# Loads of w_in in written order, |w| of the later weights on VectorE, and g2's tap and edges on GpSimd, in a three-layer float32 kernel

## The chip, the cores and the metric

The kernel runs on one core of a Trainium2 chip. The metric is device time in microseconds (us) for one execution. PE is TensorE, DVE is VectorE, ACT is ScalarE, POOL is GpSimd and SP is SyncE, whose queue issues nearly all transfers.

## The reference

Three layers follow each other, for 4 batches of 576 positions and 512 channels (8 heads of 64):

```python
# layer 1: attention, causal, window 128, with a linear bias per head
scores = scale * q @ k.T
scores = where((rel >= 0) & (rel < 128), scores + bias, -1e9)
attn = exp(scores - max); attn = attn / (attn.sum(-1) + 1e-9)
x = attn @ v                                    # heads side by side: 576 x 512
# layer 2: gated MLP with a spatial gate
h = gelu(x @ w_in)                              # 512 x 1024
u, v = h[..., :512], h[..., 512:]
v_n = (v - mean) / sqrt(var + 1e-6) * g_ln
v_s = w_sg @ v_n + b_sg                         # over the positions
x = x + (u * v_s) @ w_out
# layer 3: gated linear unit with a convolution over 3 positions
h = relu(x @ w_in2)                             # 512 x 1024
conv = conv_w[0] * h[s-1] + conv_w[1] * h[s] + conv_w[2] * h[s+1]
out = (h * sigmoid(conv)) @ w_out2              # 1024 x 512
```

The weights come in 64-bit floats; all else is float32.

## The kernel before

**Precision.** Each float32 operand of layers 2 and 3 is held as a high and a low part in a shorter float format, and a product is made of three matmuls (high by high, low by high, high by low). The names carry it: `xh`/`xl`, `gh`/`gl`, `vn`, `x2g` (high and low of the input of layer 3), `gr` (the 64 positions left over of `gg`, called the edge).

**Weights.** `narrowed` (L244 to L262) takes a piece of a 64-bit weight by DMA (L249), makes |w| from its high words (on ACT at L255 or on DVE at L257, by booked load), clamps it (L259) and puts sign and bits together in three more DVE operations (L260 to L262). The high part is then written on POOL (L181), the low part is a subtraction, mostly on POOL (L187). `w_in` comes in 8 pieces of 512 columns: `i1.k` are the halves that V uses, `i0.k` those that U uses. `w_out` has 8 pieces (`o`), `w_in2` and `w_out2` 32 pieces of 256 columns (`a`), which are written to DRAM (L308) and read back (L595) as the tiles `w2` and `wout2` when layer 3 needs them; in the trace tiles of `w_in2` read as `w`.

**Layer 1.** Heads go in pairs, four pairs a batch. L loads k and q (L321), M loads V (L325), C makes the scores on PE (`sc`, 20 matmuls a pair), DVE adds the bias and takes the maximum (L360), E takes exponentials on ACT (`t`), N norms, T transposes, A multiplies by V, X splits the result.

**Layer 2.** V.j makes `psv` and v (gelu on ACT, norm on DVE and POOL), U makes `psu` and u, G multiplies by `w_sg` (`pss`), W by `w_out` (`pso`) and writes the result x to DRAM (L549).

**Layer 3.** It reads x back (`x2s`, L607) and splits it into `x2g`. D (function `g2`) makes one block of 128 of the 1024 columns of h: 24 matmuls into `psg` (`psg2` in the program), relu into `hb`, the middle tap of the convolution (`scaled`, L198), two more taps on DVE (L645, L646), sigmoid on ACT, `gg` on DVE, its split into `gh` and `gl`, and the split of the edge into `gr0` and `gr1`. F (`g3`) multiplies by `w_out2`. There are 8 D units in each of 4 batches; three D units of batch 0 are run ahead, inside layer 2.

**Order.** Steps are written out by a list (`_steps`): batch 0's attention stands alone at the start; that of batch b+1 is woven into layer 2 of batch b. A list scheduler then moves instructions on each engine, except those that `tc.keep_in_program_order` holds. Which engine takes a flexible operation is chosen among those that the table `ON` allows, by booked loads. The stages of 64-bit pieces of `w_in` (tag `vn`) have 5 buffers, those of the smaller pieces 2, and each DMA waits for its buffer in SP's one queue.

The first steps as they are written:

```python
s = ["k0", "L0.0", "k2", "k1", "M0.0"] + scores(0) + loads(1) + ["i1.0"] + weigh(0) + scores(1) + loads(2) + ["i1.1"] + weigh(1)
...
s += back(2) + halves(2) + back(3) + halves(3) + ["k3"] + [f"i0.{k}" for k in range(4)]
```

Of the kernel before, what the change touches and what calls it, by code (L numbers as in the profile page):

```python
# [31 lines left out]
NA = 6  # L32
SLACK = 6000.0
# [6 lines left out]
    "tap": "act dve pool", "glu": "dve", "a hi": "act", "a lo": "pool",  # L40
    "edge hi": "act dve pool", "edge lo": "dve",
# [6 lines left out]
def _steps():  # L48
# [26 lines left out]
    s += back(2) + halves(2) + back(3) + halves(3) + ["k3"] + [f"i0.{k}" for k in range(4)]  # L75
    for b in range(B - 1):
# [5 lines left out]
        uv = V[:2] + loads(p) + scores(p) + V[2:] + loads(p + 1) + scores(p + 1) + U[0] + loads(p + 2) + U[1][:1] + scores(p + 2) + U[1][1:]  # L82
# [29 lines left out]
def attention_gmlp_glu_kernel(  # L112
# [185 lines left out]
    def w2_piece(i, c):  # L298
# [458 lines left out]
```

## Time and profile before

| | |
|---|---|
| median of 3 runs | 615.66 us (614.83 to 617.19) |
| profiled execution, its own time | 614.43 us |
| its span, first to last instruction | 612.4 us |
| mean granted clock of PE | 0.975 |
| PE busy | 562.5 us (92%) |
| DVE busy | 399.1 us (65%) |
| ACT busy | 244.7 us (40%) |
| POOL busy | 256.2 us (42%) |

The profile is of one execution. A busy time sums the instructions of an engine; what a wait costs is read from the stretch in which it stands. The times of the views below count from the start of the span.

### The profile page before, as it was taken

The page shows a single profiled execution, that of the slowest core. Times are in us where ns is not written, and L with a number is a line of the kernel's source. Part 1 is how long each engine was busy: PE and PEld are TensorE (multiplying, and loading weights), DVE is VectorE, ACT ScalarE, POOL GpSimd, SP SyncE. Part 2 cuts the span into 40 slices and gives each one's busy share as a digit, 9 for nine tenths or more (in the row PEclk, how much of TensorE's full clock was granted, in tenths as well). Part 3 has the DMA queues.
Part 4 walks back from the last instruction along what each step waited for, and adds up shares of the span by engine and source line. Part 5 has one row for each costly group of instructions (what it writes and reads, how often), then busy time and mean ns, then how long its engine had stood idle before and what let it go on. Part 6 is the DMA issues. An engine that isn't in the chain of part 4 may idle for free.

```text
span 612.4 us, 10380 instructions
## 1 busy us (share of the span) xinstructions
PE 562.5 (92%) x3704; PEld 480.4 (78%) x3704; DVE 399.1 (65%) x981; ACT 244.7 (40%) x626; POOL 256.2 (42%) x403
## 2 busy tenths in 40 slices
PE   6499959799998999999999997996899999999998
PEld 3366649588778888779798897886789898998887
DVE  3877957454585885586875855759996666556600
ACT  4764107863026744127733211115445333334311
POOL 0763655962142741245542634425664223322310
PEclk9799969899999899999999999997999999999999
DMA  8733402141324144424235847662200100000011
GB/s 303 278 119 102 144 2 89 40 137 33 105 100 129 45 156 128 134 58 125 66 110 152 313 136 227 206 222 78 78 17 35 55 17 18 36 18 17 18 51 52
DMA packets 44851, 63.55 MB, mean 104 GB/s; under 512 B 4352, under 2 KB 27392, under 8 KB 44800
## 3 DMA queue, kind: packets, MB, share of 16 engines
q1 hardware_dynamic: 44656, 62.60, 31.5%
q8 instruction: 29, 0.48, 0.3%
q10 hardware_dynamic: 144, 0.29, 0.1%
q14 instruction: 22, 0.18, 0.1%
HBM read 45.05 MB, written 17.83 MB: 103 GB/s over the span
## 4 chain that ended last, share of the span: by engine, by line
PE 56%; DVE 17%; DMA 12%; POOL 5%; issue 4%; ACT 4%; SPq 0%; POOLq 0%; DVEq 0%; ACTq 0%
PE psg L168 26%; PE pso L168 6%; PE o L168 6%; PE sc L168 4%; PE psv L168 4%; PE pss L168 4%; DMA w<-in_w_in_dram 4%; PE pT L402 3%; DMA w<-in_w_out_dram 3%; DVE t L360 3%; DMA w2d<-w 3%; ACT t L142 2%; PE psu L168 2%; DVE wa L261 1%; DVE wa L259 1%
## 5 line engine op out<-in xcount | busy, mean ns | idle before, releaser
L168 PE MATMUL psg<-x2g,w 128*128 128x288 f32 x768 | 108.3, 297 | 0.1
L168 PEld LDWEIGHTS psg<-x2g,w 128*128 128x128 f32 x768 | 105.8, 190 | 2.1 <-ACT hb L641 0.3
L168 PE MATMUL psg<-wout,gh 128*128 128x512 f32 (+1 forms) x272 | 82.4, 387 | 8.0 <-ACT gh L177 8.0
L142 ACT ACTIVATE t<-t,mx 128x256 f32<-128x256 f32 (+1 forms) x144 | 67.2, 469 | 23.2 <-DVE mx L360 23.1
L168 PE MATMUL pss<-wsg,vn 128*128 128x256 f32 (+1 forms) x448 | 66.4, 304 | 7.0 <-DVE t L529 7.0
L168 PEld LDWEIGHTS pss<-wsg,vn 128*128 128x128 f32 x448 | 61.9, 194 | 8.7 <-DVE t L529 8.1
L168 PE MATMUL sc<-k,q 64*128 64x256 f32 (+2 forms) x320 | 53.7, 408 | 11.8 <-DMA q<-in_q_dram 6.3
L168 PEld LDWEIGHTS psg<-wout,gh 128*128 128x128 f32 x272 | 49.8, 190 | 18.8 <-ACT gh L177 8.9
L168 PE MATMUL psu<-xh,win 128*128 128x256 f32 (+1 forms) x256 | 54.9, 307 | 8.7 <-POOL win L181 5.9
L360 DVE CUSTOM_DVE_ANT_0 t<-sc,tab 128x256 f32<-128x256 f32 (+2 forms) x144 | 47.8, 379 | 17.3 <-PE sc L168 17.2
L168 PE MATMUL pso<-gh,wo 128*128 128x256 f32 (+1 forms) x256 | 55.0, 308 | 4.1 <-DVE t L529 1.6
L198 POOL TENSOR_SCALAR t<-t,r 128x256 f32<-128x256 f32 (+2 forms) x105 | 51.3, 506 | 14.0 <-DVE r L387 6.7
L181 POOL TENSOR_SCALAR gr<-gg 128x64 fp32r<-128x64 f32 x30 | 16.4, 547 | 94.8 <-DVE gg L187 94.8
L168 PEld LDWEIGHTS sc<-k,q 64*128 64x128 f32 (+1 forms) x320 | 30.2, 198 | 32.4 <-issue 13.5
L168 PE MATMUL psg<-wout,gl 128*128 128x512 f32 (+1 forms) x136 | 52.4, 385 | 1.3 <-POOL gl L187 1.3
L168 PEld LDWEIGHTS psu<-xh,win 128*128 128x128 f32 x256 | 42.7, 196 | 11.5 <-POOL win L181 6.4
L168 PE MATMUL psv<-win,xh 128*128 128x512 f32 (+1 forms) x160 | 49.9, 397 | 0.0
L168 PEld LDWEIGHTS pso<-gh,wo 128*128 128x128 f32 x256 | 40.6, 190 | 9.0 <-DVE x L187 2.1
L187 POOL TENSOR_TENSOR gl<-gg,gh 128x512 fp32r<-128x512 f32 x32 | 43.9, 1375 | 8.2 <-ACT gh L177 8.2
L168 PE MATMUL o<-ph,V 128*64 128x128 f32 (+2 forms) x448 | 41.3, 301 | 3.1 <-ACT ph L177 2.9
L198 DVE TENSOR_SCALAR cc<-hb,cw 128x576 f32<-128x576 f32 x30 | 20.3, 680 | 30.3 <-ACT hb L641 30.3
L181 POOL TENSOR_SCALAR w<-wa 128x256 fp32r<-128x256 f32 x32 | 13.7, 428 | 62.4 <-DVE wa L262 45.6
(78 smaller groups left out, 1053.6 us busy)
## 6 DMA issues: line engine op xcount, KB each, us to landing
w<-in_w_out_dram SPq DMA_DIRECT2D x24, 256.0 KB, 2.8
V<-in_v_dram SPq DMA_DIRECT2D x16, 320.0 KB, 3.5
k<-in_k_dram SPq DMA_DIRECT2D x16, 288.0 KB, 3.1
x2s<-x2d SPq DMA_DIRECT2D x16, 288.0 KB, 2.8
q<-in_q_dram SPq DMA_DIRECT2D x15, 288.0 KB, 3.5
w<-in_w_in_dram SPq DMA_DIRECT2D x8, 512.0 KB, 7.8
w<-in_w_in_dram SPq DMA_DIRECT2D x16, 256.0 KB, 2.9
w2d<-w SPq DMA_DIRECT2D x32, 128.0 KB, 2.0
```

The source lines that it names most:

```text
L142: ins = nc.scalar.activation(*args, **kw)
L168: nc.tensor.matmul(out, lhsT, rhs, start=start, stop=stop, **kw)
L181: nc.gpsimd.tensor_scalar(dst, src, 1.0, 1.0, op0=ALU.mult, op1=ALU.mult)
L187: (nc.vector if eng == "dve" else nc.gpsimd).tensor_tensor(dst, a, b, op=op)
L198: e.tensor_scalar(dst, src, col, 1.0, op0=ALU.mult, op1=ALU.mult)
L259: tc.keep_in_program_order(clamp.tensor_scalar(f(a), f(a), W_LOW, W_HIGH, op0=ALU.max, op1=ALU.min))
L261: nc.vector.scalar_tensor_tensor(a, high, 0xC0000000, a, op0=ALU.bitwise_and, op1=ALU.bitwise_or)
L360: nc.vector.tensor_tensor_reduce(e, banks[4 if i == 4 else (j, i // 2)][:, o : o + nk], tab[:, m, tc], scale=-SCALE, scalar=3e38, op0=ALU. ...
L402: nc.tensor.transpose(ps[:, n * P : (n + 1) * P], s["t"][:, c0 : c0 + P], ident)
```

## The change

The core of the diff:

```diff
-    "tap": "act dve pool", "glu": "dve", "a hi": "act", "a lo": "pool",
-    "edge hi": "act dve pool", "edge lo": "dve",
+    "tap": "act pool", "glu": "dve", "a hi": "act", "a lo": "pool",
+    "edge hi": "pool", "edge lo": "pool",
...
-    s += back(2) + halves(2) + back(3) + halves(3) + ["k3"] + [f"i0.{k}" for k in range(4)]
+    s += back(2) + halves(2) + back(3) + halves(3) + ["k3"]
...
+        if b == 0:
+            V = [x for k in range(4) for x in (f"i0.{k}", V[k])] + V[4:]
+            uv = V + loads(p) + U[0][:1] + scores(p) + U[0][1:] + loads(p + 1) + scores(p + 1) + loads(p + 2) + U[1][:2] + scores(p + 2) + U[1][2:]
...
+    idle = mpool.tile([P, 128], BF16, tag="v", name="idle", bufs=NV)
+    nc.vector.memset(idle, 0.0)
...
-        nc.sync.dma_start(st[:, : 2 * n], src)
+        dma = nc.sync.dma_start(st[:, : 2 * n], src)
+        if stag == "vn":
+            tc.keep_in_program_order(dma)
...
-        if pick(dict(act=52 + 0.85 * n, dve=67 + 0.52 * n)) == "act":
+        if stag == "vn" and pick(dict(act=52 + 0.85 * n, dve=67 + 0.52 * n)) == "act":
             tc.keep_in_program_order(nc.scalar.activation(f(a), f(high), AF.Abs))
         else:
-            nc.vector.tensor_scalar(a, high, 0x7FFFFFFF, None, op0=ALU.bitwise_and)
+            tc.keep_in_program_order(nc.vector.tensor_scalar(a, high, 0x7FFFFFFF, None, op0=ALU.bitwise_and))
...
-        a = narrowed(src, 256, pool, "wa", 2, pool, "w64", 2)
-        hi = staged[0][:, :256].bitcast(F32R)
+        a = narrowed(src, 256, *((mpool, "v", NV) if p2pool else (pool, "wa", 2)), pool, "w64", 2)
+        hi = pool.tile([P, 256], F32R, tag="wh", name="wh", bufs=1 if p2pool else 2)
...
+            if b and (j, i) == (0, 4):
+                tc.keep_in_program_order(ins)
...
+            if b and (j, i) == (1, 0):
+                tc.keep_in_program_order(ins)
...
+    ps = gps.tile([P, 512], F32, tag="g", name="idle")
+    for _ in range(NIDLE):
+        tc.keep_in_program_order(nc.tensor.matmul(ps[:, :128], idle, idle, start=True, stop=True))
```

`NIDLE` is 40. As built, ACT carries 9 of the |w| operations instead of 36 and DVE 27 more; all 32 middle taps are on POOL (L198 becomes L203, L181 and L187 become L186 and L192), as are all edges. The high part of a `w_in2` or `w_out2` piece goes to a tile of its own (`wh`) instead of its stage.

**SP's queue at the start.** Before, the rows from the first load of `w_in` (`w64` from `in_w_in`) to the q of the third pair of heads:

```order
L249 DMA w64_140<-in_w_in_dram 128x1024
L249 DMA w64_201<-in_w_in_dram 128x1024
L249 DMA w64_262<-in_w_in_dram 128x1024
L249 DMA w64_372<-in_w_in_dram 128x1024
L560 DMA gln_80<-in_g_ln_dram 128x4
L561 DMA bsg_81<-in_b_sg_dram 128x576
L249 DMA w64_570<-in_w_in_dram 128x1024
L249 DMA w64_1796<-in_w_in2_dram 128x512
L249 DMA w64_1890<-in_w_in2_dram 128x512
L321 DMA k_195<-in_k_dram 128x576
L321 DMA q_197<-in_q_dram 128x576
```

The same place after the change:

```order
L257 DMA w64_183<-in_w_in_dram 128x1024
L577 DMA gln_80<-in_g_ln_dram 128x4
L578 DMA bsg_81<-in_b_sg_dram 128x576
L257 DMA w64_1839<-in_w_in2_dram 128x512
L257 DMA w64_1934<-in_w_in2_dram 128x512
L330 DMA k_238<-in_k_dram 128x576
L330 DMA q_240<-in_q_dram 128x576
L330 DMA k_299<-in_k_dram 128x576
L330 DMA q_301<-in_q_dram 128x576
L330 DMA k_783<-in_k_dram 128x576
L330 DMA q_785<-in_q_dram 128x576
```

Four loads of `w_in` beyond the first stood ahead of the third pair's k and q (`k_195` and `q_197`, now `k_238` and `q_240`); now the next load of `w_in` comes behind these rows and one load of V.

**ACT around the first V steps.** Before, |w| of the four `i0` pieces and the gelus of V (`v` from `psv`):

```order
L255 ACTIVATE wa_572<-w64_570 128x512
L255 ACTIVATE wa_582<-w64_580 128x512
L255 ACTIVATE wa_592<-w64_590 128x512
L255 ACTIVATE wa_602<-w64_600 128x512
L142 ACT_TABLE_LOAD
L142 ACTIVATE v_624<-psv_610 128x512
L142 ACTIVATE v_650<-psv_636 128x512
L177 CAST wsg0_666<-wst_790 128x576
L177 CAST wsg0_666<-wst_848 128x576
L142 ACTIVATE v_716<-psv_702 128x512
L142 ACTIVATE v_742<-psv_728 128x512
```

After the change, from the first gelu to the first u:

```order
L147 ACTIVATE v_637<-psv_623 128x512
L147 ACTIVATE v_673<-psv_659 128x512
L147 ACTIVATE v_709<-psv_695 128x512
L147 ACTIVATE v_745<-psv_731 128x512
L264 ACTIVATE wa_651<-w64_649 128x512
L264 ACTIVATE wa_687<-w64_685 128x512
L147 ACTIVATE v_771<-psv_757 64x512
L264 ACTIVATE wa_723<-w64_721 128x512
L147 ACTIVATE u_808<-psu_795 128x256
```

Before, all four |w| stood ahead of the first gelu; now one of them (`wa_615`) does, and the other three stand behind the fourth gelu, the last of them behind the fifth.

**DVE and POOL at the first D units that follow layer 2.** Before, DVE's rows from the third `gg` on (`cc` is the convolution's sum, `gr1` the low part of the edge):

```order
L187 TENSOR_TENSOR gg_4759<-cc_4754,hb2_4641 128x576
L187 TENSOR_TENSOR gr1_4686<-gg_4679,gr0_4685 128x64
L187 TENSOR_TENSOR gr1_4686<-gg_4720,gr0_4685 128x64
L198 TENSOR_SCALAR cc_4793<-hb0_4639,cw_82 128x576
L198 TENSOR_SCALAR cc_4832<-hb1_4640,cw_82 128x576
L187 TENSOR_TENSOR gr1_4686<-gg_4759,gr0_4685 128x64
L645 SCALAR_TENSOR_TENSOR cc_4793<-hb0_4639,cw_82,cc_4793 128x576
L645 SCALAR_TENSOR_TENSOR cc_4832<-hb1_4640,cw_82,cc_4832 128x576
```

After the change, POOL's rows at that place:

```order
L203 TENSOR_SCALAR cc_4829<-hb2_4716,cw_82 128x576
L186 TENSOR_SCALAR x2g_5049<-x2s_5051 128x576
L186 TENSOR_SCALAR gr0_4760<-gg_4754 128x64
L192 TENSOR_TENSOR gr1_4761<-gg_4754,gr0_4760 128x64
L192 TENSOR_TENSOR gl_4757<-gg_4754,gh_4756 128x512
L203 TENSOR_SCALAR cc_4868<-hb0_4714,cw_82 128x576
L186 TENSOR_SCALAR gr0_4760<-gg_4795 128x64
L192 TENSOR_TENSOR gl_4798<-gg_4795,gh_4797 128x512
L186 TENSOR_SCALAR gr0_4760<-gg_4834 128x64
L203 TENSOR_SCALAR cc_4907<-hb1_4715,cw_82 128x576
```

The taps (`cc` from `hb`) and the low edges (`gr1`) left DVE and stand on POOL between the high edges (`gr0`) and `gl`.

On PE the three D units that are run ahead move forward in V of batch 3: before, 6 of their 72 matmuls stood ahead of the fifth `psv` group and the rest among U and G; now 54 of them stand ahead of the third `psv` group, and the other 18 between the fourth and the fifth.

## Rows read from the trace of the kernel before

**Rows 1.** Windows: length, busy us of each engine, granted clock, DMA share, GB/s.

```profile
0.00:20.00 20.00, 10.08 (x40) 5.55 (x40) 9.48 (x44) 9.69 (x33) 4.12 (x13) 0.97 0.92 324
...
60.00:80.00 20.00, 16.01 (x92) 10.97 (x90) 20.00 (x70) 3.04 (x5) 13.63 (x16) 1.00 0.35 113
...
80.00:95.00 15.00, 10.06 (x57) 9.17 (x57) 7.00 (x14) 2.63 (x7) 5.62 (x10) 0.66 0.00 0
...
120.00:340.00 220.00, 214.98 (x1562) 180.80 (x1559) 149.83 (x468) 96.84 (x284) 92.85 (x169) 0.99 0.34 107
...
400.00:420.00 20.00, 14.29 (x97) 13.67 (x95) 14.35 (x23) 9.00 (x15) 5.79 (x13) 0.86 0.61 201
...
420.00:450.00 30.00, 26.34 (x166) 23.86 (x165) 29.30 (x37) 12.40 (x22) 20.54 (x19) 0.98 0.17 48
```

**Rows 2.** Timeline, PE and ACT at the start: start, duration, operation, [idle before].

```profile
5.28 5.01 PE L168 MATMUL sc<-k,q 64*64 64x192 f32 x20 [5.28 <-DMA k<-in_k_dram]
...
10.50 5.07 PE L168 MATMUL sc<-k,q 64*64 64x192 f32 x20 [0.21 <-DMA q<-in_q_dram]
...
12.76 0.66 ACT L255 ACTIVATE wa<-w 128x512 f32<-128x512 f32 x1 [2.20 <-DMA w<-in_w_in_dram]
...
71.11 2.69 PE L168 MATMUL sc<-k,q 64*64 64x192 f32 x20 [0.19 <-DVE mx L360]
```

**Rows 3.** Chain of waits, first 125 us: start, duration, what.

```profile
6.63 8.68 DMA w<-in_w_in_dram
...
15.33 6.23 DMA q<-in_q_dram
...
87.62 11.36 PE psu L168 x72
```

**Rows 4.** Timeline, PE at the first U steps.

```profile
77.47 0.50 PE L168 MATMUL psu<-xh,win 128*128 128x256 f32 x2 [2.05 <-POOL win L181]
...
84.55 0.80 PE L168 MATMUL psu<-xh,win 128*128 128x256 f32 x2 [3.88 <-POOL win L181]
```

**Rows 5.** Timeline, SP, DVE, ACT and PE from 334 to 380 us.

```profile
335.98 3.21 SPq L595 DMA_DIRECT2D w<-w2d  x6
...
364.88 0.29 DVE L257 TENSOR_SCALAR wa<-w 128x256 uint32<-128x256 uint32 x1 [2.21 <-DMA w<-in_w_out_dram]
...
376.05 0.43 ACT L255 ACTIVATE wa<-w 128x256 f32<-128x256 f32 x1 [3.60 <-DMA w<-in_w_out_dram]
...
378.38 2.32 PE L168 MATMUL pss<-wsg,vn 128*128 128x320 f32 x14 [3.09 <-DVE t L529]
```

**Rows 6.** Timeline, POOL and PE at the change to layer 3.

```profile
412.03 0.67 POOL L181 TENSOR_SCALAR x2g<-x2s 128x576 fp32r<-128x576 f32 x1 [7.87 <-DMA x2s<-x2d]
...
418.13 2.07 PE L168 MATMUL psg<-wout,gh 128*128 128x512 f32 x4 [5.71 <-ACT gh L177]
```

**Rows 7.** Lines by form, 405 to 450 us: busy, mean ns, idle before.

```profile
L187 POOL TENSOR_TENSOR gl<-gg,gh 128x512 fp32r<-128x512 f32 x9 | 14.2, 1592 | 0.0
...
L645 DVE SCALAR_TENSOR_TENSOR cc<-hb,cw,cc 128x576 f32<-128x576 f32 x10 | 9.3, 950 | 0.6 <-POOL cc L198 0.6
...
L187 DVE TENSOR_TENSOR gr<-gg,gr 128x64 fp32r<-128x64 f32 x9 | 7.3, 827 | 0.1
...
L187 DVE TENSOR_TENSOR gg<-cc,hb 128x576 f32<-128x576 f32 x9 | 6.7, 753 | 0.0
...
L198 DVE TENSOR_SCALAR cc<-hb,cw 128x576 f32<-128x576 f32 x6 | 6.1, 1029 | 0.0
...
L198 POOL TENSOR_SCALAR cc<-hb,cw 128x576 f32<-128x576 f32 x2 | 2.6, 1309 | 0.0
```

**Rows 8.** One tile's view, gr on DVE: nanoseconds minimum, median, maximum.

```profile
L187 DVE TENSOR_TENSOR gr<-gg,gr x32: 211/1284/1322, 419.4 to 582.6; 128x64 fp32r<-128x64 f32 x32
```

**Rows 9.** Timeline, POOL and DVE at 445 us.

```profile
445.07 1.28 POOL L187 TENSOR_TENSOR gl<-gg,gh 128x512 fp32r<-128x512 f32 x1
...
445.14 1.29 DVE L187 TENSOR_TENSOR gr<-gg,gr 128x64 fp32r<-128x64 f32 x1
```

More of the change, by code (lines that the diff above doesn't have):

```diff
@@ L32 @@
 NA = 6
+NIDLE = 40
 SLACK = 6000.0
@@ L81, in _steps @@
         W = [[f"W{b}.{half}.{m}" for m in range(4)] for half in range(2)]
-        uv = V[:2] + loads(p) + scores(p) + V[2:] + loads(p + 1) + scores(p + 1) + U[0] + loads(p + 2) + U[1][:1] + scores(p + 2) + U[1][1:]
+        if b == 0:
+            V = [x for k in range(4) for x in (f"i0.{k}", V[k])] + V[4:]
+            uv = V + loads(p) + U[0][:1] + scores(p) + U[0][1:] + loads(p + 1) + scores(p + 1) + loads(p + 2) + U[1][:2] + scores(p + 2) + U[1][2:]
+        else:
+            uv = V[:2] + loads(p) + scores(p) + V[2:] + loads(p + 1) + scores(p + 1) + U[0] + loads(p + 2) + U[1][:1] + scores(p + 2) + U[1][1:]
         T, A = ([f"{x}{of(p + i)}" for i in range(4)] for x in "TA")
@@ L87, in _steps @@
         if b == 0:
-            s += weave(uv, [f"g{c}" for c in range(5)] + [f"o{k}.0" for k in range(4)]) + ["o0.1"] + gw[:2] + ["o1.1"] + gw[2:4] + ["o2.1"] + gw[4:6] + ["o3.1"] + gw[6:]
+            s += uv[:9] + weave(uv[9:], [f"g{c}" for c in range(5)] + [f"o{k}.0" for k in range(4)]) + ["o0.1"] + gw[:2] + ["o1.1"] + gw[2:4] + ["o2.1"] + gw[4:6] + ["o3.1"] + gw[6:]
         else:
@@ L167, in mm @@
         load["pe"] += book_pe
-        nc.tensor.matmul(out, lhsT, rhs, start=start, stop=stop, **kw)
+        return nc.tensor.matmul(out, lhsT, rhs, start=start, stop=stop, **kw)
     def copy(dst, src, psum=False, engines="act dve pool"):
@@ L241, in attention_gmlp_glu_kernel @@
     kept = {}
-    staged = []
     STAGE = dict(st=S, vn=1024, w64=512)
@@ L248, in narrowed @@
         st = spool.tile([P, STAGE[stag]], U32, tag=stag, name="w64", bufs=sbufs)
-        nc.sync.dma_start(st[:, : 2 * n], src)
-        staged[:] = [st]
+        dma = nc.sync.dma_start(st[:, : 2 * n], src)
+        if stag == "vn":
+            tc.keep_in_program_order(dma)
         words = st[:, : 2 * n].rearrange("p (n w) -> p n w", w=2)
@@ L353, in block @@
             out = banks[of][d if i == 4 else slice(0, P), o : o + nk]
-            mm(out, s["q"][d, q0 : q0 + nq], s["k"][d, k0 : k0 + nk], start=True, stop=True)
+            ins = mm(out, s["q"][d, q0 : q0 + nq], s["k"][d, k0 : k0 + nk], start=True, stop=True)
+            if b and (j, i) == (0, 4):
+                tc.keep_in_program_order(ins)
         def masked(j, i):
             o, nk = BLK[i][6], BLK[i][3]
-            e, c, tc = weights(s, j, i)
+            e, c, part = weights(s, j, i)
             book("dve", 80 + nk)
-            nc.vector.tensor_tensor_reduce(
-                e, banks[4 if i == 4 else (j, i // 2)][:, o : o + nk], tab[:, m, tc],
+            ins = nc.vector.tensor_tensor_reduce(
+                e, banks[4 if i == 4 else (j, i // 2)][:, o : o + nk], tab[:, m, part],
                 scale=-SCALE, scalar=3e38, op0=ALU.add, op1=ALU.min, accum_out=s["mx"][:, c : c + 1],
             )
+            if b and (j, i) == (1, 0):
+                tc.keep_in_program_order(ins)
         for j, i in ((0, 4), (1, 0), (0, 0), (1, 1), (0, 1)):
```

## The prediction

> **What bounds the kernel now.** I read the windows first. From 120 to 340 us PE is busy 214.98 of 220 us at a clock of 0.99, so there nothing but PE's own work could be saved beyond 5.0 us [rows 1]. The losses stand at two places. One is the first 95 us: PE idles 9.9 us of the first 20, 4.0 us from 60 to 80, and 4.9 us from 80 to 95, where the granted clock is 0.66, part of it at 1.2 GHz instead of 2.4. The other is the change to layer 3: 5.7 us idle from 400 to 420 and 3.7 us from 420 to 450 [rows 1]. In both, DVE is full beside an idle PE: 20.00 of 20 us from 60 to 80, 29.30 of 30 us from 420 to 450.
>
> Then the timeline of the start. The first 20 score matmuls take 5.01 us and the next 5.07 us; the same 20 take 2.69 us at 71 us [rows 2]. The ratio of 1.9 is near that of the two clock levels, though the window's clock column reads 0.97 there; I trust the durations. ACT's |w| of a `w_in` piece at 12.76 us stands among the exponentials and holds them for 2.20 us [rows 2]. The chain of waits then runs through a transfer of w_in from 6.63 us (8.68 us long) into the load of the third pair's q, which lands at 15.33 + 6.23 = 21.6 us. Its last step in this stretch is a run of 72 U matmuls from 87.62 to 98.98 us [rows 3].
>
> At 77.47 and 84.55 us U waits 2.05 and 3.88 us for `win`, the pieces i0 of w_in that POOL narrows late [rows 4]. Late in layer 2 a chain of the same kind shows once: |w| on ACT at 376.05 us, the load before it 3.60 us late, then PE at 378.38 us, idle 3.09 us [rows 5].
>
> At the change to layer 3 the first read of x lands at about 412 us, and PE resumes with `gh` at 418.13 us after 5.71 us of idleness [rows 6].
>
> **The change part by part.** The sum is made against the profiled execution's 614.43 us, which is 1.2 us under the median of 615.66 us.
>
> *Warm-up matmuls.* No row shows a 128-column matmul of this kind. The 72 U matmuls of 256 to 320 columns take 158 ns each, some cold [rows 3]; by columns that is 65 ns for 128, twice that cold, so 40 take 2.6 to 5.2 us. Begun at 1 us (a guess, no row shows it) they end between 3.6 and 6.2 us, and the first scores start at 5.28 us now, since they wait for k: nothing to 0.9 us lost. If the clock then stays up, the first scores save 5.01 - 2.69 = 2.3 us. The second 20 save as much, but behind them stands the third pair's q, so that is not added.
>
> The Trainium skill, page "TensorE: Matmul & The Clock Gate", Part 1 on the clock gate, gives 107 ns between cold matmuls of 128 columns; by it the estimate is 40 x 0.107 = 4.3 us and no delay.
>
> *Loads of w_in in written order.* Four pieces of 512 KB leave SP's queue ahead of the third pair's k and q. That is 2.1 MB; at the first window's 324 GB/s it is 6.5 us [rows 1], and the long load's own 8.68 us for what was queued with it is the upper bound [rows 3]. I take 5.5 us, as that window includes the 2 us before any load ran: q lands near 16 us instead of 21.6 us. Less if k and q then wait for their buffers, which the faster first scores free earlier. The exponentials of the pairs that follow start earlier by that, and the 2.20 us before 12.76 us fall away inside it.
>
> *i0 among the V steps.* Attention of batch 0 then ends earlier, and DVE, full from 60 to 80 us, has the same work: what starts 5.5 us earlier ends so. But three of the four |w| of i0 now stand on ACT behind the fourth gelu, where before all stood ahead of the first. What queues behind them is their clamp on DVE, the high part on POOL, and U on PE. If they come early enough, U's waits of 2.05 and 3.88 us go, and half of the 11.36 us run no longer runs cold (2 us more). If they come late, the lead is eaten. I take the lead of the load plus 1 us of U: **-6.5 us** (bounds: -14, all of the waits and the cold run gone; +2, three pieces of about 2 us each in series behind the last gelu, less the lead).
>
> *|w| of the later weights on DVE.* It is 27 more instructions of 0.29 us on DVE [rows 5], 7.8 us, hidden where DVE is idle (70 of 220 us from 120 to 340 [rows 1]). The exponentials lose the weights between them. From 120 to 340 PE can gain 5.0 us at most; I take **-1** (0 to -4). At 376 us the wait was for a load that stands behind larger loads of `wout`; with the high part in a tile of its own a stage comes free one POOL step earlier and the load is issued before them: **-2** (0 to -3.09).
>
> *D units run ahead.* 54 of their matmuls now follow two V groups of batch 3 instead of 6 following four. The loads of w2 are issued from 335.98 us [rows 5], behind the last part written to DRAM; two V groups are 24 matmuls of 512 columns, by the U run's 158 ns for some 290 columns [rows 3] about 7 us of PE. So that much of the cover that the loads had is gone: **+1** (0 to +7, if PE must wait for all but its first parts).
>
> *Tap and edges to POOL.* Now the DVE group from 405 to 450 us: nine units (the nine `gg`), with the low edge at 827 ns and six taps at 1029 ns; POOL's `gl` takes 1592 ns and its tap 1309 ns [rows 7]. DVE gives away about 0.83 + 0.69 = 1.5 us a unit. POOL, busy 20.54 of 30 us [rows 1], takes on at least 1.31 + 0.21 us a unit. Nine units in those 45 us are 5.0 us each; POOL's 20.54/30 of that, 3.4 us, plus 1.5 us is 4.9 us. One full engine is traded for another. Yet the low edge has two lengths, 211 ns at least and 1284 ns in the median [rows 8], and at 445.14 us it lasts just as long as the `gl` beside it [rows 9]: the two take turns, and on one engine that wait is gone. Bounds: -9.4 us if both waits of PE go (5.7 + 3.7), +5 if POOL's rows grow by a third of what it takes on. I take **-1.5**.
>
> Sum: -6.5 - 1 - 2 + 1 - 1.5 = -10, which is 604.4 us for the profiled execution and **605.5 us** on the median's scale.
>
> **The rivals.**
> *The lead is swallowed.* The three |w| behind the gelus set U's end, and the run of 72 still ends near 99 us. For it: DVE has no idle time from 60 to 80 us [rows 1]. Against: 5.5 us of DVE's work moves ahead. Without the 6.5 us: 612 us.
>
> *Everything comes.* U's waits go (2.05 + 3.88 us on top of the lead) and the first D units run at PE's pace (9.4 us instead of 1.5): 605.5 - 5.9 - 7.9 = 591.7 us. For it: DVE is full exactly where PE idles.
>
> *The w2 loads hold PE.* The full 7 us instead of 1: 611.5 us.
>
> *POOL and DVE exclude each other (slower).* The place is the D units from 402 us on. Rows 9 show one such turn. If it held for all of POOL's work and DVE's three operations over two tiles, a unit would take 1.31 + 0.21 + 0.24 + 1.28 on POOL plus two of 0.95 and 0.75 (and about as much for `x2g`) on DVE: 6.4 us, 0.24 being the high edge, taken a little over the low one's minimum. Nine take 57.6 us instead of 45: 605.5 + 1.5 + 12.6 = 619.6 us. It decides above 6.3 us a unit, where nine take 11.7 us more than now and use up the 8.5 us of the other terms and 3.1 us (0.5%) more. Against: `gg` with 753 ns in the mean can hardly hold turns of 1.28 us, and the low edge, which does, leaves DVE.
>
> The Trainium skill, page "SBUF — State Buffer", section "Who interferes with whom", states such a rule: a VectorE instruction with two inputs in SBUF and a GpSimd instruction that reads SBUF share a port pair, and the later one fully waits. Rows 9 agree with it; whether it holds so strictly for the long operations the rows leave open.
>
> **How the numbers follow.** About 0.5% is what a measurement of this kernel can tell from no change, so faster means under 612.6 us, slower over 618.7 us. Forecast 0.48 (its own range 598 to 611.5); lead swallowed 0.15; everything 0.17; w2 loads 0.09; exclusion 0.11. Faster: nearly all of the forecast, half of the swallowed, all of the next and two thirds of the w2 case: 0.46 + 0.08 + 0.17 + 0.06 = 0.77. Slower: 0.1, most of the exclusion. The rest, 0.13, is no change. The range reaches from everything (591) to the swallowed lead with a little exclusion (615).
>
> **What would show it.** First scores near 2.7 us and the third pair's q landing near 16 us show the start right. The U run ending at 92 to 93 us instead of 99 shows that the lead came through; waits of U on `win` behind ACT's |w| would show it swallowed. No idle PE at 376 us. In V of batch 3, PE waiting on transfers of w2 would be the w2 case. In the D units, POOL near 5 us a unit with PE idle 6 to 9 us from 400 to 450 is the forecast; more idle there is the exclusion, less is the gain. The prediction is wrong if the scores stay at 5 us (then it was not the clock), if the third pair's loads wait for buffers, or if a unit goes over 6.3 us.

## The result and the profile after

The changed kernel takes 620.96 us (median of 7 runs, 618.1 to 623.1) where the kernel before takes 615.87 us in the same series. The ratio is 1.007, with a 95% interval of 1.0045 to 1.0096: 0.7% slower (ratios, here and below, leave disturbed runs out, so they can differ a little from the quotient of two medians). The forecast was 605.5 us. The profiled execution took 618.1 us, its span is 616.3 us.

Where the time went is read by putting the same points of the program side by side: the start of the first instruction of each kind on PE, in the timelines of the two profiled executions.

| point of the program | before, us | after, us | after - before |
|---|---|---|---|
| last step of U done, first `pss` of batch 0 | 98.81 | 105.05 | +6.2 |
| first `pso` of batch 0 | 107.81 | 116.47 | +8.7 |
| first `psv` of batch 3 | 331.99 | 330.95 | -1.0 |
| first D unit behind layer 2 | 402.66 | 405.99 | +3.3 |
| first F matmul | 418.13 | 418.76 | +0.6 |
| end of the span | 612.4 | 616.3 | +3.9 |

So the lead of 6.5 us that was forecast for U's end is a loss of 6.2 us; the middle gives back nearly ten; and layer 3 with V of batch 3 ahead of it loses five again. The windows of the kernel after, with the columns of [rows 1]:

```profile
0.00:20.00 20.00, 14.01 (x98) 10.33 (x98) 10.79 (x52) 10.60 (x39) 5.83 (x16) 0.93 0.76 259
...
60.00:80.00 20.00, 13.43 (x53) 9.68 (x51) 15.55 (x29) 3.61 (x6) 11.33 (x19) 0.76 0.08 27
...
400.00:420.00 20.00, 16.55 (x115) 15.81 (x114) 14.95 (x26) 7.51 (x13) 8.92 (x17) 1.00 0.56 184
420.00:450.00 30.00, 25.18 (x142) 23.14 (x142) 25.37 (x24) 12.53 (x21) 29.92 (x30) 0.83 0.21 62
```

Against [rows 1]: PE does 3.9 us more in the first 20 us (the warm-up alone is 4.45 us), but from 60 to 80 us it is busy 13.4 us instead of 16.0, DVE 15.6 instead of 20.0, and the clock there is 0.76. From 420 to 450 us POOL is now the full engine, 29.92 of 30 us, and PE is worse off: 25.18 us busy at a clock of 0.83, with 142 matmuls done where the kernel before did 166 at 0.98.

The start itself went as forecast, up to a point. PE's timeline, with the 40 matmuls first:

```profile
1.00 4.45 PE L566 MATMUL idle<-idle 128*128 128x128 bf16 x40 [1.00 <-DVE idle L242]
5.38 3.38 PE L173 MATMUL sc<-k,q 64*64 64x192 f32 x20
10.66 2.90 PE L173 MATMUL sc<-k,q 64*64 64x192 f32 x20 [1.90 <-DMA q<-in_q_dram]
16.65 4.31 PE L173 MATMUL sc<-k,q 64*64 64x192 f32 x20 [3.10 <-DMA q<-in_q_dram]
```

The matmuls end at 5.45 us and hold the first scores up by no more than 0.1 us (5.38 us, before 5.28). The first pair's scores take 3.38 us instead of 5.01, and the third pair's, which began at about 21.7 us, begin at 16.65 us: k and q land 5 us earlier, as the queue's bytes said. Attention of batch 0 ends earlier too: its last product with V (`o`) is done at 48.8 us instead of 55.3. But this is SP's queue behind them:

```profile
5.31 0.71 SPq L257 DMA_DIRECT2D w<-in_w_in_dram  x1
...
29.40 0.55 SPq L334 DMA_DIRECT2D V<-in_v_dram  x1
30.00 0.62 SPq L257 DMA_DIRECT2D w<-in_w_in_dram  x1
...
38.55 0.55 SPq L334 DMA_DIRECT2D V<-in_v_dram  x1
39.15 1.58 SPq L257 DMA_DIRECT2D w<-in_w_in_dram  x3
```

The second load of w_in is issued at 30.00 us and three more at 39.15 us, each right behind a load of V, which waits for a V buffer that PE has yet to read out. In the kernel before, seven of the eight loads of w_in had been issued by 21.5 us. So the pieces of V's half (`i1`) reach DVE late, and V waits for them. U waits too:

```profile
73.35 0.80 PE L173 MATMUL psu<-xh,win 128*128 128x256 f32 x2 [3.49 <-POOL win L186]
...
81.88 0.80 PE L173 MATMUL psu<-xh,win 128*128 128x256 f32 x2 [2.49 <-POOL win L186]
```

The waits of 3.49 and 2.49 us answer to those of [rows 4]. What sets the last piece stands on ACT and in SP's queue:

```profile
66.33 1.22 ACT L264 ACTIVATE wa<-w 128x512 f32<-128x512 f32 x2
...
75.80 0.70 ACT L264 ACTIVATE wa<-w 128x512 f32<-128x512 f32 x1 [6.61 <-DMA w<-in_w_in_dram]
```

```profile
72.29 0.33 SPq L257 DMA_DIRECT2D w<-in_w_in_dram  x1
```

Two |w| of `i0` come right behind the fourth gelu. DVE narrows these two pieces until 72.2 us; only then is a stage free, and the eighth load of w_in is issued at 72.29 us. Its |w| follows at 75.80 us, DVE and POOL finish the piece, and PE takes it up at 83.69 us, 2.7 us before its time in the kernel before. Behind it the chain of waits holds what before had been done elsewhere:

```profile
83.69 0.80 PE psu L173 x2
84.48 4.69 PE sc L173 x20
89.17 3.30 PE psu L173 x26
92.48 2.67 PE sc L173 x20
```

All three pairs of scores that the new order weaves in (`sc` x20) stand among U's matmuls behind the last piece: at 84.41 us (4.76 us long, at the low clock), 92.41 and 98.77 us (2.72 us each), 10.2 us of PE together. Before, these scores ran among the V steps, from 53 to 73 us, and in [rows 3] the run behind the last piece is U's alone. From the last piece to U's end PE needs 21.4 us instead of 12.5 us, 8.9 us more; less the lead of 2.7 us, that is the loss of 6.2 us.

In V of batch 3 PE waits for the read-back of w2, and at the change to layer 3 and in the D units behind it for `gh` and `gl`:

```profile
340.23 1.02 PE L173 MATMUL psg<-x2g,w 128*128 128x288 f32 x6 [3.63 <-DMA w<-w2d]
```

```profile
418.76 1.20 PE L173 MATMUL psg<-wout,gh 128*128 128x512 f32 x4 [3.02 <-ACT gh L182]
...
439.29 0.51 PE L173 MATMUL psg<-wout,gl 128*128 128x512 f32 x1 [2.21 <-POOL gl L192]
```

The wait at the change has fallen from 5.71 us [rows 6] to 3.02 us, but those for `gl` are new. The groups from 405 to 450 us, with the columns of [rows 7]:

```profile
L192 POOL TENSOR_TENSOR gl<-gg,gh 128x512 fp32r<-128x512 f32 x8 | 14.4, 1797 | 0.0
...
L663 DVE SCALAR_TENSOR_TENSOR cc<-hb,cw,cc 128x576 f32<-128x576 f32 x9 | 11.3, 1252 | 0.1
L192 DVE TENSOR_TENSOR gg<-cc,hb 128x576 f32<-128x576 f32 x8 | 9.8, 1229 | 0.5 <-ACT cc L147 0.5
```

POOL's `gl` takes 1797 ns where it took 1592, and on DVE it is now `gg` that lengthened, from 753 ns [rows 7] to 1229 ns. Over all 32 of them (tile view: minimum, median, maximum in ns), before and after:

```profile
L187 DVE TENSOR_TENSOR gg<-cc,hb x32: 746/758/786, 416.7 to 581.4; 128x576 f32<-128x576 f32 x32
```

```profile
L192 DVE TENSOR_TENSOR gg<-cc,hb x32: 746/1030/1850, 416.5 to 583.8; 128x576 f32<-128x576 f32 x32
```

A long one, with the `gl` beside it:

```profile
426.12 1.80 POOL L192 TENSOR_TENSOR gl<-gg,gh 128x512 fp32r<-128x512 f32 x1
```

```profile
426.69 1.84 DVE L192 TENSOR_TENSOR gg<-cc,hb 128x576 f32<-128x576 f32 x1
```

`gl` ends at 427.92 us and this `gg` at 428.53 us, 0.6 us later: it fits a `gg` that begins, waits for `gl` and then does most of its 0.75 us of work.

The middle is the good part: the wait of 3.09 us at 378 us [rows 5] is gone, and between the first `pso` of batch 0 and V of batch 3 the kernel after needs 214.5 us instead of 224.2 us.

### The profile page after: what moved, and what is told of

Read it like the earlier page. It is cut to its first block, busy times and chain, and to the rows that moved or that the text cites. A ratio compares the mean times of both kernels' runs of the same rounds, so it can differ in the third digit from the quotient of the medians.

```text
span 616.3 us, 10420 instructions
## 1 busy us (share of the span) xinstructions
PE 565.9 (92%) x3744; PEld 488.1 (79%) x3744; DVE 385.2 (63%) x949; ACT 235.9 (38%) x598; POOL 301.5 (49%) x464
## 4 chain that ended last, share of the span: by engine, by line
PE 59%; POOL 11%; DVE 11%; DMA 7%; issue 5%; ACT 4%; SPq 2%; POOLq 0%; ACTq 0%
PE psg L173 26%; PE psu L173 7%; PE psv L173 6%; PE sc L173 6%; PE pso L173 5%; PE o L173 4%; PE pss L173 3%; POOL gl L192 3%; PE pT L415 2%; ACT t L147 2%; DMA w<-in_w_out_dram 2%; DMA w<-in_w_in_dram 2%; DVE t L203 2%; POOL cc L203 1%; DVE wa L270 1%
## 5 line engine op out<-in xcount | busy, mean ns | idle before, releaser
L173 PE MATMUL psg<-x2g,w 128*128 128x288 f32 x768 | 110.7, 304 | 3.8 <-DMA w<-w2d 3.8
L173 PEld LDWEIGHTS psg<-x2g,w 128*128 128x128 f32 x768 | 109.1, 196 | 6.2 <-ACT v L147 4.0
L203 POOL TENSOR_SCALAR t<-t,r 128x256 f32<-128x256 f32 (+2 forms) x105 | 54.4, 536 | 25.1 <-DVE r L400 18.9
L662 DVE SCALAR_TENSOR_TENSOR cc<-hb,cw,cc 128x576 f32<-128x576 f32 x32 | 28.4, 891 | 49.2 <-POOL cc L203 49.2
L173 PE MATMUL psv<-win,xh 128*128 128x512 f32 (+1 forms) x160 | 53.2, 411 | 5.2 <-POOL win L186 3.2
L173 PE MATMUL sc<-k,q 64*128 64x256 f32 (+2 forms) x320 | 49.3, 390 | 5.0 <-DMA q<-in_q_dram 5.0
L192 DVE TENSOR_TENSOR gg<-cc,hb 128x576 f32<-128x576 f32 x32 | 35.5, 1109 | 21.1 <-ACT cc L147 21.0
L173 PEld LDWEIGHTS sc<-k,q 64*128 64x128 f32 (+1 forms) x320 | 29.9, 194 | 22.4 <-issue 11.6
L203 POOL TENSOR_SCALAR cc<-hb,cw 128x576 f32<-128x576 f32 x32 | 30.1, 944 | 34.4 <-ACT hb L658 34.4
L192 POOL TENSOR_TENSOR gl<-gg,gh 128x512 fp32r<-128x512 f32 x32 | 45.9, 1436 | 2.1 <-ACT gh L182 2.1
L186 POOL TENSOR_SCALAR wh<-wa 128x256 fp32r<-128x256 f32 x32 | 14.1, 441 | 62.5 <-DVE wa L271 46.8
```

Source lines behind the costliest of these rows:

```text
L173: return nc.tensor.matmul(out, lhsT, rhs, start=start, stop=stop, **kw)
L186: nc.gpsimd.tensor_scalar(dst, src, 1.0, 1.0, op0=ALU.mult, op1=ALU.mult)
L192: (nc.vector if eng == "dve" else nc.gpsimd).tensor_tensor(dst, a, b, op=op)
L203: e.tensor_scalar(dst, src, col, 1.0, op0=ALU.mult, op1=ALU.mult)
L662: nc.vector.scalar_tensor_tensor(cc, h[:, 0:S], cw[:, 0, c : c + 1], cc, op0=ALU.mult, op1=ALU.add)
```

## The experiments

Each was timed in five rounds beside the kernel before on the same chip; the ratio is to that kernel, its 95% interval in brackets. "Alone" means: on the kernel before, nothing else changed. The views are of one execution of each kernel, so a point in them can lie off the median: with the old start and free scores, e18 aside, U ends at 98.8 to 101.0 us in ten traces, but at 103.0 us in e7's, whose time of 622.7 us is the longest of e7's executions.

| run | what it is | median, us | ratio |
|---|---|---|---|
| e4 | \|w\| on DVE, pinned, alone | 610.67 | 0.9898 [0.9874, 0.9922] |
| e18 | \|w\| on DVE, not pinned, alone | 649.47 | 1.0515 [1.0470, 1.0559] |
| e8 | e4 with own tile and shared buffer | 612.62 | 0.9942 [0.9922, 0.9962] |
| e16 | e4 with shared buffer only | 617.56 | 1.0008 [0.9989, 1.0028] |
| e17 | e4 with own tile in the first segment only | 611.73 | 0.9921 [0.9893, 0.9949] |
| e14 | e8 with the first D units late | 616.34 | 0.9982 [0.9961, 1.0003] |
| e15 | e4 with the first D units late | 610.99 | 0.9892 [0.9859, 0.9925] |
| e3 | tap and edges as changed, alone | 620.43 | 1.0067 [1.0042, 1.0091] |
| e11 | e4 with the edges on POOL | 614.08 | 0.9943 [0.9916, 0.9970] |
| e6 | pins on the scores alone | 621.77 | 1.0092 [1.0068, 1.0115] |
| e10 | pin on w_in's loads alone | 621.83 | 1.0065 [1.0029, 1.0101] |
| e7 | warm-up alone | 617.53 | 1.0012 [0.9986, 1.0038] |
| e2 | changed, tap and edges undone | 619.47 | 1.0015 [0.9982, 1.0048] |
| e1 | changed, order of steps and loads' pin undone | 624.68 | 1.0121 [1.0086, 1.0155] |
| e5 | changed, scores' pins undone | 625.55 | 1.0151 [1.0115, 1.0188] |
| e13 | changed, loads' pin undone | 623.81 | 1.0105 [1.0071, 1.0140] |
| e9 | changed, whole start undone but the warm-up | 618.59 | 1.0031 [1.0007, 1.0056] |
| e12 | changed, tap, edges and tile undone | 616.97 | 0.9960 [0.9927, 0.9992] |

**The start or layer 3?** The first four runs took the two places apart. e1 undoes the order of the first steps and the pin on the loads:

```diff
-    s += back(2) + halves(2) + back(3) + halves(3) + ["k3"]
+    s += back(2) + halves(2) + back(3) + halves(3) + ["k3"] + [f"i0.{k}" for k in range(4)]
...
-        if stag == "vn":
-            tc.keep_in_program_order(dma)
```

> The changed kernel with the order of the first steps and the free order of w_in's transfers as before; all else as changed. Theory Q (the loss is at the start: w_in's loads stand in SP's queue behind loads of V that wait for buffers, and batch 1's scores behind U's waits): the end of U moves from 105.1 us to at most 96, and the kernel gains 4 to 9 us on the changed one: 612 to 617 us. Rival P (the loss is in layer 3, POOL being full): U's end moves but the 9.7 us that the middle gave back shrink with it, and the time stays within 2 us of 621.

It fell out the other way: slower still, and U's end stayed at 104.5 us. Both theories miss: without this part the kernel is 0.5% slower, hardly clear of noise, so the part cannot be where the loss sits, unless with the pins on the scores, which this run still has. e2 and e3 take the table's rows:

```diff
-    "tap": "act pool", ...
-    "edge hi": "pool", "edge lo": "pool",
+    "tap": "act dve pool", ...
+    "edge hi": "act dve pool", "edge lo": "dve",
```

> The changed kernel with the table's rows for tap and edges as before; all else as changed. Theory P (POOL's share of g2 costs): from the first F matmul to the end 3 us less (191 instead of 194 us), clock in 420 to 450 us back above 0.95, 617 to 618 us. Theory Q: no more than 1 us off 621.

> The kernel before with only the table's rows for tap and edges changed. Theory P: 3 us slower, near 619 us, lost from 418 us on, POOL busy over 29 of 30 us there. The forecast's term: 1.5 us faster, 614 us. If the edge moves freely: 616 us.

Undone, the ratio falls from 1.0070 to 1.0015; put alone on the kernel before it costs 0.67%, 4.1 us. Theory P holds for this part, with the sign opposite to the forecast's term. e3's window, its groups and one of PE's waits:

```profile
420.00:450.00 30.00, 24.60 (x129) 22.21 (x129) 27.17 (x26) 14.18 (x24) 29.68 (x29) 0.79 0.23 67
```

```profile
L646 DVE SCALAR_TENSOR_TENSOR cc<-hb,cw,cc 128x576 f32<-128x576 f32 x9 | 10.4, 1157 | 0.1
...
L187 DVE TENSOR_TENSOR gg<-cc,hb 128x576 f32<-128x576 f32 x8 | 9.9, 1232 | 0.0
```

```profile
444.99 0.80 PE L168 MATMUL psg<-wout,gl 128*128 128x512 f32 x1 [2.20 <-POOL gl L187]
```

The first of the two groups in the kernel before:

```profile
L646 DVE SCALAR_TENSOR_TENSOR cc<-hb,cw,cc 128x576 f32<-128x576 f32 x9 | 7.5, 852 | 0.0
```

POOL is full, PE waits for `gl`, and DVE's two long operations take 1157 and 1232 ns, where the same groups of the kernel before have 852 and 753 ns: DVE's operations now hold time that is not their own work.

e4 moves |w| and pins it:

```diff
-        if pick(...) == "act":
+        if stag == "vn" and pick(...) == "act":
...
-            nc.vector.tensor_scalar(a, high, 0x7FFFFFFF, ...)
+            tc.keep_in_program_order(nc.vector.tensor_scalar(a, high, 0x7FFFFFFF, ...))
```

> The kernel before with only |w| of the later weights on DVE. My account of the middle (the changed kernel gave back 9.7 us between the first W step and V of batch 3, of which 4 us were idle PE): 3 to 5 us faster, 611 to 613 us, with PE idle 120 to 340 us at 2 us or less. Rival: the recovery is only the work that the scores' order put elsewhere; then within 1 us of 616.

1.0% faster, 6 us: more than expected, and the fastest kernel of the study beside e15, which is level with it. PE's waits from 100 to 335 us in the kernel before (what waits, for whom: total, times, longest), the first row; and the first row of e4's:

```profile
PE pss L168 <- DVE t L529: 3.7, 3, 2.6
```

```profile
PE pso L168 <- DVE x L187: 1.7, 1, 1.7
```

In that stretch `pss` no longer waits for DVE's `t`. From the first `pso` of batch 0 to the first `psv` of batch 3, in windows of the kernel before and of e4:

```profile
107.81:331.99 224.18, 216.00 (x1575) 180.35 (x1576) 148.01 (x462) 105.10 (x320) 100.73 (x185) 0.98 0.32 98
```

```profile
108.89:326.35 217.46, 212.53 (x1575) 178.55 (x1574) 149.56 (x473) 99.47 (x304) 101.88 (x183) 0.99 0.33 101
```

Of the 6.7 us, 3.3 us are idle time of PE (8.2 to 4.9 us); the other 3.5 us are busy time, for the same 1575 matmuls at a clock of 0.99 instead of 0.98. The stretch takes 214.5 to 219.7 us in the traces of all the kernels with |w| pinned on DVE, and 223.6 to 227.9 us in those with |w| as before. (The wait at 376 us lies behind it, and e4 keeps that: 3.11 us at 372.52 us.) e18 takes the pin away and leaves |w| on DVE:

> The kernel before with |w| of the later weights on DVE but free to be moved; as built the first pieces of w_in2 are narrowed inside batch 0's attention. If the engine is what counts: 610 to 612 us as with the pin. If the pin is: 615 to 618 us, with PE's waits for DVE's t (3.7 us from 100 to 335 us before, none with the pin) back.

PE's longest waits over the whole run, first row:

```profile
PE pss L168 <- DVE t L529: 13.7, 4, 9.3
```

Without the pin the scheduler moves the first pieces of `w_in2` into batch 0's attention, ahead of pieces of w_in. DVE waits 6.9 us for their loads and is busy with their narrowing, 98.3 of the first 125 us in all; U ends at 125.0 us instead of 98.8 us, and the kernel loses 5.2%. So |w| may go to DVE only with its place held. Whether with the pin the gain comes from ACT being freed or from the held order itself no run tells apart.

**What of the start costs.** e5 and e6 take the pins on the scores of batches 1 to 3, from the changed kernel and onto the one before:

```diff
+            if b and (j, i) == (0, 4):
+                tc.keep_in_program_order(ins)
...
+            if b and (j, i) == (1, 0):
+                tc.keep_in_program_order(ins)
```

> The changed kernel without the two pins on the scores of batches 1 to 3. Undoing the order of the first steps left U's end at 104.5 us, so theory Q is shaken; theory C: the pins keep PE from taking scores one by one into V's waits and put whole pairs into U. Then U ends at 99 to 101 us and the kernel gains 3 to 5 us: 616 to 618 us. Theory Q (transfers alone): U's end stays at 104 to 106 us and the time at 621.

> The kernel before with only the two pins. Theory C: U's end goes from 98.8 to 103 or later and the kernel loses 2 to 5 us: 618 to 621 us. Theory Q: 616 us.

Alone the pins cost 0.92%, 5.7 us. e6 on PE: the last piece of w_in is there at 86.67 us, as in the kernel before, but one pair of scores follows it inside U, and U ends at 103.08 us instead of 98.81:

```profile
86.67 0.58 PE L168 MATMUL psu<-xh,win 128*128 128x256 f32 x1 [1.01 <-POOL win L187]
...
95.04 2.72 PE L168 MATMUL sc<-k,q 64*64 64x192 f32 x20
...
103.08 5.20 PE L168 MATMUL pss<-wsg,vn 128*128 128x256 f32 x42
```

The pair is 2.72 us of this. More is lost in the middle: the stretch from batch 0's `pso` to batch 3's `psv` takes 227.9 us instead of 224.2 us, and PE's wait of `pss` for DVE's `t`, 3.7 us in the kernel before, has grown in it (100 to 335 us):

```profile
PE pss L168 <- DVE t L533: 8.0, 2, 4.2
```

In the changed kernel, with |w| on DVE, the same wait is 1.5 us: this part of the pins' price does not arise there. Yet without them the changed kernel is slower, not faster: theory C holds for the pins alone, in part, and not for the whole. In e5 DVE takes the masks of batch 1 into V again, and with the pieces late anyway the last one arrives only at 92.9 us.

e10 pins the loads alone, e13 frees them in the changed kernel:

> The kernel before with only w_in's loads pinned. SP's queue then has three of the later w_in loads behind the second and third pair's loads of V. Theory Q: the pieces i1 are narrowed 15 us later, V starts no earlier than before though q lands at 16 us, U ends at 100 us or later: 617 to 620 us. Forecast's reasoning: everything 5 us earlier, 610 us.

> The changed kernel with w_in's transfers free, the new order of steps and the score pins kept. Theory Q (pinned loads behind V's loads cost, 0.65% by themselves): 617 to 618 us. Rival (with scores late the DVE has room for late pieces, and the pins fit the new order): 621 to 624 us.

e10's queue on SP, and PE at the last wait of U and at its end:

```profile
42.81 0.55 SPq L327 DMA_DIRECT2D V<-in_v_dram  x1
43.41 3.07 SPq L249 DMA_DIRECT2D w<-in_w_in_dram  x5
```

```profile
87.59 0.80 PE L168 MATMUL psu<-xh,win 128*128 128x256 f32 x2 [5.08 <-POOL win L181]
...
103.18 5.08 PE L168 MATMUL pss<-wsg,vn 128*128 128x256 f32 x41
```

Five loads of w_in stand behind the load of V that goes out at 42.81 us. The third pair's scores begin at 17.1 us, as intended, and U ends at 103.18 us: the lead of the loads is turned into a loss of 4.4 us, 0.65% on the whole. Theory Q holds for this part alone.

In e13 freeing them does not help. Five loads of w_in are out by 15.6 us, yet the last again waits for a stage until DVE has narrowed earlier pieces, 15.4 us, and the last piece and U's end stand where they stood in the changed kernel (83.69 and 105.05 us):

```profile
83.53 0.58 PE L173 MATMUL psu<-xh,win 128*128 128x256 f32 x1 [1.00 <-POOL win L192]
...
104.90 3.28 PE L173 MATMUL pss<-wsg,vn 128*128 128x256 f32 x26
```

So in the changed kernel it is not the loads behind V that set U's end. What stands ahead of it in both traces is the |w| behind the gelus, the stage of the last load, and the scores behind the last piece; no run takes these away one at a time. (The ratio of e13 is 1.0105, which is not clear of the changed kernel's 1.0070.)

So they were undone together, with only the warm-up kept:

> The changed kernel with everything of its start as before except the warm-up: order of steps, free transfers, free scores. What is left of the change are the warm-up, |w| on DVE, the own tile and POOL's share. If the parts add up (on the kernel before: |w| -1.0%, own tile +0.4%, POOL's share +0.7%, warm-up +0.1%), it stands 0.2% over the kernel before, 618 us, 3 us under the changed one, and the start costs those 3 us. Rival: the new order of steps gains, since undoing it alone cost 0.5%: then 621 us or more.

That takes the ratio from 1.0070 to 1.0031: the start as a whole costs 0.4%, 2.4 us, with an uncertainty nearly as large, and the sum of the parts, 1.002, was a fair guess. The warm-up alone:

> The kernel before with only the 40 matmuls. In the changed kernel they took 4.45 us and the first 20 scores 3.38 instead of 5.01 us. If the next load still sets the pace, nothing remains of that at U's end: within 1 us of 616. If the forecast's 2.3 us carry: 613.5 us. If the clock falls back before the second pair, the second 20 scores are again at 5 us.

```profile
5.38 2.72 PE L168 MATMUL sc<-k,q 64*64 64x192 f32 x20
11.37 4.49 PE L168 MATMUL sc<-k,q 64*64 64x192 f32 x20 [3.27 <-DMA q<-in_q_dram]
```

It speeds up the first pair (2.72 us instead of 5.01), PE then waits 3.27 us for q, and the second pair again runs at 4.49 us. Nothing is left of it: 1.0012, an interval that holds 1.

**V of batch 3.** e8 adds to e4 the high part's own tile, and with it the buffer of `v` that the narrowed piece takes in the last segment:

```diff
-        a = narrowed(src, 256, pool, "wa", 2, pool, "w64", 2)
-        hi = staged[0][:, :256].bitcast(F32R)
+        a = narrowed(src, 256, *((mpool, "v", NV) if p2pool else (pool, "wa", 2)), pool, "w64", 2)
+        hi = pool.tile([P, 256], F32R, tag="wh", name="wh", bufs=1 if p2pool else 2)
```

> The kernel before with |w| on DVE (610.7 us by itself) and the high part in a tile of its own. With that tile PE's order puts 54 matmuls of the first D units ahead of the third V group of batch 3. Theory W: PE waits there 3 to 4 us for w2 and the gain of |w| shrinks to 613 to 615 us. Rival: the wait only moves idle time that came later; 610 to 611 us.

It costs 0.44%, 2.7 us. To see whether the wait for w2 was the reason, the early D units were pinned behind the first U matmul of batch 3 (`PINU`), with and without the tile:

> The kernel before with |w| on DVE, the own tile, and the first three D units pinned behind U of batch 3's first matmul; as built they then run behind layer 2 altogether. Theory W (the tile's loss is PE's wait for w2): the 3.6 us wait and the 3.1 us wait near 375 us are both gone, 608 to 610 us against 612.6. Rival: D units that start later bring the convolution's chain later, and the change to layer 3 loses what is gained: 612 us or more.

> As e14 without the own tile. Theory W: the wait of 3 us near 375 us is back, 1 to 3 us slower than e14. Rival (the tile itself costs): faster than e14.

Theory W falls. e14 is slower than e8, and PE has a longer wait at the same place, for another thing:

```profile
349.85 1.11 PE L169 MATMUL psv<-win,xh 128*64 128x512 f32 x2 [12.11 <-ACT v L143]
```

V's gelu, not the D units, holds PE there: with the units moved away PE waits all the same. e16 keeps only the shared buffer, e17 only the tile, in the first segment:

> The kernel before with |w| on DVE, the high part in the stage as before, and the narrowed pieces of the third segment in buffers of v. Theory V (the shared buffers hold the gelus of V of batch 3 back): 2 to 4 us over |w| alone, 613 to 615 us, with the same PE wait of 3 to 4 us at the D units. Rival (own tile): 610.7 us.

> The kernel before with |w| on DVE and the own tile in the first segment alone, no buffers shared. Theory V: no loss against |w| alone, 609.5 to 611.5 us, and no wait at the D units. Rival (own tile): 613 us.

e16 on PE and on ACT:

```profile
334.94 10.09 PE L168 MATMUL psg<-x2g,w 128*128 128x288 f32 x54 [3.21 <-DMA w<-w2d]
```

```profile
349.11 0.60 ACT L142 ACTIVATE v<-psv 128x512 f32<-128x512 f32 x1 [16.57 <-DMA w2d<-wa]
```

The gelu of V of batch 3 waits, 16.57 us idle on ACT, until a narrowed piece (`wa`) has been written to DRAM and its buffer is free. That write goes out at 347.29 us, because DVE could begin the piece only at 341.91 us: its load was issued at 333.64 us, among eight reads of w2 of 512 KB each.

```profile
341.91 0.29 DVE L257 TENSOR_SCALAR wa<-w 128x256 uint32<-128x256 uint32 x1 [6.81 <-DMA w<-in_w_out_dram]
```

In e16, without the new tile, 54 matmuls of the first D units stand ahead of the third `psv` group, as in e8; in e17, with the tile and no sharing, they do not. So the shared buffer puts the D units there. e8 and e14 have the same kind of idle time ahead of that gelu (17.34 and 16.76 us). Theory V holds: the shared buffer costs 1.1% over e4 (0.9898 to 1.0008), while e17, with the own tile and no sharing, is level with e4 within the intervals. e8, with both, loses less (0.44%); there the own tile has taken away PE's wait for DVE's `t` near 376 us, which is 1.94 us in e16, but what the rest of the difference is no run shows. What e17 loses by keeping the old stage at the end is small; its wait for DVE's `t` is 2.42 us:

```profile
371.88 3.86 PE L168 MATMUL pss<-wsg,vn 128*128 128x320 f32 x14 [2.42 <-DVE t L529]
```

**What a better version would keep.** e11 puts the edges alone on POOL, e12 takes the changed kernel without POOL's share and the tile:

> The kernel before with |w| on DVE and both edges on POOL, the tap left as before (DVE mostly). The low edge took turns with gl on DVE (1.28 us instead of 0.21); on POOL it is 0.25 us in line. Theory P says the tap is what fills POOL: 1 to 2 us faster than |w| alone, 609 us. If any move to POOL costs: 612 us.

> The changed kernel with tap and edges and the high part's place as before; what is left are |w| on DVE, the warm-up, and the whole new start with its pins. If the parts add up: 621 less 3.4 less 2.7 us, 615 us, still 4 us over |w| alone (610.7), and these 4 us are the start's. Rival: without w2's wait the start's shape does not matter: 611 us.

The edges alone cost 0.45% too, though on DVE each took turns with `gl`: on POOL the low edge takes 751 ns in the mean (405 to 450 us), three times the 0.25 us expected, and DVE's `gg` there 1055 ns. The forecast of 609 us failed. e12 stands 0.6% over e4, a little more than the start's 0.4% in e9. The version to keep is e4: the kernel before with |w| of the later weights on DVE at a held place, 610.67 us, and none of the other parts.

## Why the prediction was wrong

*Step that failed first: "Attention of batch 0 then ends earlier, and DVE ... has the same work: what starts 5.5 us earlier ends so."* The first half came true. The second failed at U: the last piece of w_in came only 2.7 us earlier. Three |w| stand behind the fourth gelu, and the eighth load, which needs a stage, could go out only when DVE had narrowed earlier pieces (72.29 us). Then 10.2 us of scores stood behind the last piece, where before there were none, and the trace shows U's end 6.2 us later. The term was -6.5 us; the whole start measures +2.4 us (e9).

*The queue, counted in bytes.* The text did not ask what w_in's own loads now stand behind. Loads that had gone out by 21.5 us went out at 30.0 and 39.2 us, behind loads of V that wait for a buffer; V has two, as was to be read from the program. Alone this costs 0.65% (e10). In the changed kernel it is not what U's end hangs on: with the loads free, it stays (e13).

*A part costed at nothing: the pins on the scores.* The prediction does not speak of them. Alone they cost 5.7 us (e6): 2.7 us of it is a pair of scores moved behind the last piece, and the middle, where `pss` waits longer, loses more. In the changed kernel the waits in the middle are short, and taking the pins away makes it slower, as the last piece then comes at 92.9 us (e5).

*"The lead is swallowed"* was the rival with 0.15, at 612 us. It named the three |w| behind the gelus. They came at 66.3 and 75.8 us and did hold U up; but they left 2.7 us of the lead, and what turned it into a loss were the scores behind the last piece, which no rival named.

*|w| on DVE: a right direction, mis-sized.* For the middle -1 us was forecast (0 to -4); e4 measures -6.3 us by its ratio. The 5 us of idle PE from 120 to 340 us were taken as the limit. The idle time gave 3.3 us; the busy time of the same matmuls shrank as well, by 3.5 us, and that was left out. The pin, on which all of it depends (e18), was not mentioned.

*The tile for the high part: -2 us forecast.* The wait near 376 us is indeed gone where the tile is (the changed kernel, e8, e14) and stays where it is not (3.11 us in e4). But with the tile came the borrowed buffers of `v`, and the two together cost 2.7 us (e8).

*D units run ahead: +1 us.* The wait for w2 is there (3.63 us at 340.23 us), inside the bounds of 0 to 7. But the units stand there for the borrowed buffer (e16 has them there, e17 not), and V of batch 3 could not go on without them either: its gelu waits for a buffer that the change had lent to the narrowed pieces (e14, e16). What a tile's new pool already holds was not looked up.

*Tap and edges: -1.5 us, measured +3.4 (e2) to +4.1 us (e3).* The sum said that one full engine was traded for another, and still took a gain. The sign that it named for the forecast came, POOL near 5 us a unit (eight `gl` in 45 us) with 8.3 us of idle PE from 400 to 450 us; the loss shows in the matmuls done (142 for 166) and the clock (0.83 for 0.98). The rival of exclusion had the mechanism right: DVE's long two-input operations lengthened (753 to 1229 ns, 852 to 1252 ns) once POOL was full. The argument against it, that `gg`'s mean could hardly hold such turns, was drawn from a POOL that was idle a third of the time. The Trainium skill, page "SBUF — State Buffer", section "Who interferes with whom", says that a VectorE instruction with two SBUF inputs and a GpSimd instruction that reads SBUF contend for a port pair, which one of them holds at a time. The trace agrees in direction, with `gg` at up to 1850 ns beside `gl` and never above 786 ns before; the price measured is below the 12.6 us that the rival took for turns at every operation.

*Warm-up:* the spacing of 111 ns (4.45 us for 40) lies inside the bounds, and no delay followed; the saving at the first pair came, and nothing carried it on (e7).

The parts, as measured: start +2.4, |w| -6.3, tile with shared buffer +2.7, POOL's share +3.4 to +4.1 us. They add up to +2.2 to +2.9 us, where +4.3 us (2.8 to 5.9) was measured; what is left is within the uncertainty of four differences. Open stays how the parts of the start act on each other: the loads alone cost (e10) and freeing them gains nothing (e13), the scores' pins alone cost (e6) and undoing them costs too (e5). For the pins the waits in the middle explain a part; the rest no run settles, only the sum.

## What to carry to other kernels

Before moving a load back in a queue, look at what it then stands behind: a load that waits for a buffer stops everything after it, and bytes do not show that. Then look at what else stands between the last transfer and the point that is to move: here it was work on two engines and three pairs of scores. When work is moved off an engine that is full, add up the engine that takes it, and take instructions that grow longer beside it as a sign that the two share something; such waits move along with the work. A pin or a borrowed buffer is a change of its own and wants its own price: here |w| on DVE gained six microseconds with its place held and lost over thirty without.

## What the runs showed of the hardware

The 40 matmuls of 128 columns were spaced at 111 ns in the kernel after. The first 20 scores behind them took 3.38 us there, but 2.72 us in e7 with the same 40 ahead: the same lead-in does not buy the same. DVE's `gg` of one shape takes 753 ns in the mean (405 to 450 us) where POOL is busy 20.5 of the 30 us from 420 to 450 us, 1055 ns in e11 where it is busy 26.3 us, and 1229 or 1232 ns where it is busy 29.9 or 29.7 us. In e2, with POOL busy 17.9 us there, six of them still take 1006 ns in the mean, but the median of all 32 is 758 ns, as in the kernel before (in the kernel after it is 1030 ns).
